# Logits in column quarters behind the turn, 0/1 products in column halves, a reordered start

One NeuronCore of one Trainium2 chip. The metric is device time in microseconds (us), lower is better. The experiments ran on two chips, called 2 and 3 here; which chip the first runs of the kernel before and the changed one used is not on record (it is called the first). On chips 2 and 3 these two kernels took 0.7 to 0.9% longer, so kernels are compared on one chip, or by their ratio to the kernel before on the same chip.

The profiler names the engines: PE is TensorE, which multiplies matrices (PEld its loads of the stationary side), DVE is VectorE, ACT is ScalarE, POOL is GpSimd, SP issues transfers (DMA). "The array" is PE's array. A row "PE sc <- DVE pr: 2.0, 2, 1.7" means that PE products into `sc` waited for DVE's `pr` for 2.0 us in all, 2 times, 1.7 us at the longest; a bracket "[1.71 <-DVE pr]" is the engine's idle time just before a row and what ended it.

## The reference

```python
# attention: B=8, H=8, S=576, head 64; heads 0-3 a window of 32, heads 4-7 every 4th of 128
scores = where(mask, q @ k.T / 8, -1e9);  x = softmax(scores) @ v       # x: (8, 576, 512)
# mixture of experts, 8 experts, hidden size 1024
logits = x @ w_gate;  local = sigmoid(x @ w_local)
for each token in order:
    e = argmax(logits) if first of its row or local < 0.5 else the previous token's e
    out = softmax(logits)[e] * (relu(x @ w1[e]) @ w2[e])
```

All products are f32. A token's expert can depend on its predecessors, so the routing of a group (two batch rows, 1152 tokens) is a chain of small steps. They run beside the attention of later groups: as the program is built, each small step is put into a `gap` between pieces of TensorE work, counted in planned us.

## The kernel before

Parts that the change touches (cuts are marked `# ...`):

```python
def load(n):                                 # keys+queries, the mask once, values of head pair n
    nc.sync.dma_start(out=kq, in_=qk[n])
    if not n: nc.sync.dma_start(out=mk, in_=mask)
    nc.sync.dma_start(out=vt[...], in_=v[n]) # ...
def idle():                                  # products of zeros, ahead of scores 0
    zeros = bank([P, 4, P], "idle")
    for i in range(2): nc.tensor.matmul(zeros, lhsT=blank, rhs=...)   # 128x128 by 128x512
idle(); load(0); load(1)                     # ... and idle() once more behind scores 0
def logits(g):                               # three thirds of 384 tokens in three column groups of 32
    lps = [bank([P, NQ], "lp") for _ in range(2)]        # the middle third's two pieces lie in two banks
    for kk in range(DK):
        for lp, b, c, s, z in sorted(parts, ...):
            nc.tensor.matmul(lp[c*LW:(c+1)*LW, ...], lhsT=wg[:, kk], rhs=..., tile_position=(0, c*LW))
    for lp, b, c, s, z in parts: nc.scalar.copy(le[...], lp[...])     # 4 copies
def put(lv, g):                              # places of tokens: product of two 0/1 matrices
    for j in range(NJ):                      # NJ = 9
        nc.tensor.matmul(tp, lhsT=by_place[:, j], rhs=by_tile[:, j], ...)
def gap(us):                                 # "planned work" passes; at most one small step goes in
    gaps[0] += us
    if soon: soon.pop(0)()
    elif waiting and gaps[0] - last[0] >= waiting[0][0]:
        last[0] = gaps[0]; waiting.pop(0)[1]()
def route(g):
    soon.append(lambda: logits(g))
    steps = [(2.0, fresh), (4.0, carry), (2.0, carry_over), (1.2, choose), (2.7, place), (0.8, gate)]
    waiting.extend(...)                      # then table, seek, and for each group mark and put, then gathers
```

A head pair's `scores` are followed by a DVE clamp (`pr`), an ACT exponential, and `values` (`pv`); two pairs are turned (`tp`) and copied by ACT to `xt`, from which the logits are made. Experts: gather (`xg`), transposes (`tp`), hidden layer (`hp`), output (`yp`).

Of the kernel before, what the change touches and what calls it, by code (L numbers as in the profile page):

```python
# [10 lines left out]
F32 = mybir.dt.float32  # L11
BF16 = mybir.dt.bfloat16
# [10 lines left out]
P = 128  # L23
B, H, S, DH = 8, 8, 576, 64
# [4 lines left out]
WIN, DIL = 32, 4  # L29
# [3 lines left out]
QB = 64  # L33
NB = S // QB
KW = QB + WIN
# [6 lines left out]
CH = 2  # L42
# [3 lines left out]
GB = 2  # L46
NG = B // GB
GS = GB * S
TB = 128
NJ = GS // TB  # L50
NC = 3
NQ = GS // NC
LW = 32
# [9 lines left out]
HALF = P // 2  # L63
# [212 lines left out]
def whole(ctx, tc, exact, qk, v, wgl, w1, w2, con, msk, qmk, out, cst, wg, ones, xd, kept, register):  # L276
    nc = tc.nc
    ctx.enter_context(tc.manual_schedule(engines={ET.PE}))

    def pool(name, bufs, **kw):  # L280
        return ctx.enter_context(tc.tile_pool(name=name, bufs=bufs, **kw))
# [4 lines left out]
    once = pool("once", 1)  # L286
# [4 lines left out]
    ins, work, xp, xtp, marks, mp = (pool(name, bufs) for name, bufs in (  # L291
        ("ins", 4 if exact else 5), ("work", 3), ("xp", 4), ("xtp", 3), ("marks", 2), ("mp", 2)))

    def bank(shape, name):
        return banks.tile(shape, F32, name=name, tag="bank")
# [5 lines left out]
    loaded = {}  # L301

    vts = [once.tile([KW, 2, NB, VW], F32, name=f"vt{i}") for i in range(ahead + 1)]
    for vt in vts:
        nc.vector.memset(vt[:WIN, :, 0], 0.0)

    def load(n):
        kq = ins.tile([P, WIN + 2 * S], F32, name="kq")
        vt = vts[n % len(vts)]
        nc.sync.dma_start(out=kq, in_=qk[n])  # L310
        if not n:
            nc.sync.dma_start(out=mk, in_=mask)
        nc.sync.dma_start(out=vt[WIN:].rearrange("p u i e -> p (u i e)"), in_=v[n])
        loaded[n] = kq[:, :WIN + S], kq[:, WIN + S:], vt

    def nobody():

# [10 lines left out]
        engine = nc.vector if n >= NPB - 7 else nc.gpsimd  # L328
        engine.tensor_copy(vt[:WIN, :, 1:], vt[QB:, :, :NB - 1])  # L329

    def idle():

        zeros = bank([P, 4, P], "idle")
        for i in range(2):
            nc.tensor.matmul(zeros, lhsT=blank, rhs=blank.unsqueeze(1).to_broadcast([P, 4, P]),  # L335
                             start=True, stop=True, skip_group_check=True)

    if not exact:
        blank = once.tile([P, P], F32, name="blank")
        nc.vector.memset(blank, 0.0)  # L340

        idle()
    mk, mask = once.tile([P, QB + 2 * NB * KW] if exact else [KW, 2 * S], BF16, name="mk"), qmk if exact else msk
    load(0)
    load(1)
    if not exact:
        nc.sync.dma_start(out=cst, in_=con)
        nc.sync.dma_start(out=wg.rearrange("p k e -> p (k e)"), in_=wgl)
# [121 lines left out]
    def logits(g):  # L470

        st = routes[g]

        lps = [bank([P, NQ], "lp") for _ in range(2)]
        parts = []
        for c in range(NC):
            at = [(b, c, max(c * NQ, b * S), min((c + 1) * NQ, (b + 1) * S)) for b in range(GB)]
            parts += [(lp, *p) for lp, p in zip(lps, [p for p in at if p[2] < p[3]])]
        for kk in range(DK):
            for lp, b, c, s, z in sorted(parts, key=lambda p: p[0] is lps[1]):  # L480
                nc.tensor.matmul(lp[c * LW:(c + 1) * LW, s - c * NQ:z - c * NQ], lhsT=wg[:, kk],  # L481
                                 rhs=st["xt"][b][:, kk // CH, s - b * S:z - b * S, kk % CH], start=(kk == 0),
                                 stop=(kk == DK - 1), skip_group_check=True, tile_position=(0, c * LW))
        st["le"] = le = sm.tile([NC * LW, NQ], F32, name="le")
        for lp, b, c, s, z in parts:
            w = slice(c * LW, (c + 1) * LW)
            nc.scalar.copy(le[w, s - c * NQ:z - c * NQ], lp[w, s - c * NQ:z - c * NQ])

    def fresh(g):

# [249 lines left out]
    def loads(lv):  # L740

        return 2 if lv == len(GROUPS) - 1 else TW
# [18 lines left out]
    def put(lv, g):  # L761

        by_place, by_tile = tiles.pop("marks")
        nt = COLS[lv]
        tp = bank([P, loads(lv), nt], "put")
        for j in range(NJ):
            nc.tensor.matmul(tp, lhsT=by_place[:, j], rhs=by_tile[:, j], start=(j == 0), stop=(j == NJ - 1))  # L767
        if not g:
            tiles["there", lv] = once.tile([P, loads(lv), nt], F32, name=f"there{lv}")
            nc.vector.tensor_copy(tiles["there", lv], tp)  # L770
        else:
            nc.vector.tensor_tensor(tiles["there", lv], tiles["there", lv], tp, op=Alu.add)
        if g < GROUPS[lv] - 1:
            return
        for w, (what, nobody) in enumerate((("tok", N), ("gate", 0), ("plain", ROWS), ("dilated", ROWS))):
            tiles[what, lv] = to = (kept[what] if loads(lv) == 2
                                    else once.tile([P, nt], I32 if nobody else F32, name=f"{what}{lv}"))
            if w < loads(lv):
                nc.vector.tensor_scalar(to, tiles["there", lv][:, w], float(nobody), None, Alu.add)
        if loads(lv) == 2:  # L780
            rows(lv)
        named[0] = NT if lv else EARLY
# [33 lines left out]
    def pieces(a, z):  # L816
        order = [(t, second) for t in range(a, z) for second in (False, True)]

        for t in (ps[1] + 1 for _, _, ps in TILES if len(ps) > 1):
            if a <= t < z - 1:  # L820
                i = order.index((t, True))
                order[i:i + 2] = order[i + 1], order[i]
        return [(*k, c) for k in order for c in range(PC)]

    needs = pieces(0, TILES[LAST][2][0])
# [3 lines left out]
    def fetch(most):  # L829
        for _ in range(min(most, len(needs))):  # L830
            t, second, _ = needs[0]
            if t >= known[0] or (t >= 2 and t - 2 not in (outs if second else hid)):
                return
            weights(*needs.pop(0))

    def weights(t, second, c):

        if not second and not c:
            at = t - EARLY * (t >= EARLY)
            ev[t] = nc.values_load(tiles["experts", int(t >= EARLY)][0:1, at:at + 1], engines=[ET.SP], min_val=0, max_val=E - 1,  # L840
                                   skip_runtime_bounds_check_because="clamped to the experts")
        w, s, pattern = ((w2, w2s, "p m f -> p (m f)") if second else (w1, w1s, "p m k f -> p (m k f)"))
        cond = {} if t < 2 else dict(cond=ev[t] != ev[t - 2], cond_hint=False)
        m = FK // PC
        nc.sync.dma_start(out=s[t % 2][:, c * m:(c + 1) * m].rearrange(pattern),
                          in_=w[bass.ds(ev[t], 1), c].rearrange("o p x -> (o p) x"), **cond)


    gaps, sent = [0.0], {}
# [98 lines left out]
    waiting, last, soon = [], [0.0], []  # L948

    def gap(us):  # L950
        gaps[0] += us
        if soon:
            soon.pop(0)()
        elif waiting and gaps[0] - last[0] >= waiting[0][0]:
            last[0] = gaps[0]
            waiting.pop(0)[1]()

    def route(g):

        soon.append(lambda: logits(g))  # L960
        steps = [(2.0, fresh), (4.0, carry), (2.0, carry_over), (1.2, choose), (2.7, place), (0.8, gate)]
        lv = GROUPS.index(g + 1) if g + 1 in GROUPS else None
        if lv is not None:
            steps.insert(5, (0.0, lambda g: table(lv)))
            steps.append((1.2, lambda g: seek(lv)))

        waiting.extend((us if g + 1 == GROUPS[0] else 2 * us, lambda f=f: f(g)) for us, f in steps)
        if lv is not None:
            for h in range(g + 1):
                waiting.append((2.5, lambda h=h: mark(lv, h)))  # L970
                waiting.append((6.5 if h else 9.0, lambda h=h: put(lv, h)))
            waiting.extend((1.2, lambda t=t, kk=kk: begin(t, kk))
                           for t in range(EARLY * lv, EARLY * lv + 3) for kk in range(DK))
# [27 lines left out]
    begun = [0]  # L1001
# [14 lines left out]
    for n in range(NPB + 2):  # L1016
        if n < NPB:
            overlap(n)
            (scores_exact if exact else scores)(n)
            if not n and not exact:  # L1020
                idle()
        gap(0.9)
        step()
        if n >= 2 and n % 2 == 1:
            turn((n - 3) // 2)
            if n >= 3 and (n - 3) // 2 % (2 * GB) == 2 * GB - 1:
                route((n - 3) // 2 // (2 * GB))
            gap(0.8)
        if 1 <= n <= NPB:
            values(n - 1)  # L1030
            gap(0.6)
        step()
        if n + ahead < NPB:
            load(n + ahead)
        fetch(1 if not begun[0] else 6)
        if n == NP:
            nobody()
        if n >= 3 and n % 2 == 1:
            store((n - 3) // 2)
        step()  # L1040
# [75 lines left out]
```

## Time and profile before

| kernel before, first chip | |
|---|---|
| median of runs | 726.13 us (724.15 to 727.18, four runs) |
| profiled run | 727.98 us, span 726.2 us |
| TensorE (PE) busy | 709.1 us, 98% |
| attention and start | to 148.6 us; the first expert's hidden layer starts there |
| experts alone | a tile each 14.45 us, to 718 us; then the last write |

In a profile a product's row lasts to the modelled end of its pipeline, so starts of instructions tell more than busy shares (in the profile before, rows of L931 last 593 ns in the mean, and start 429 ns apart in the median): what a piece of work costs the array is the time from its first start to the first start of the next piece. A stop of PE measured by starts is likewise some 0.2 us longer than the idle time in a bracket (1.9 and 1.71 us for the same stop below).

### The profile page before, as it was taken

The page shows a single profiled execution, that of the slowest core. Times are in us where ns is not written, and L with a number is a line of the kernel's source. Part 1 is how long each engine was busy: PE and PEld are TensorE (multiplying, and loading weights), DVE is VectorE, ACT ScalarE, POOL GpSimd, SP SyncE. Part 2 cuts the span into 40 slices and gives each one's busy share as a digit, 9 for nine tenths or more (in the row PEclk, how much of TensorE's full clock was granted, in tenths as well). Part 3 has the DMA queues.
Part 4 walks back from the last instruction along what each step waited for, and adds up shares of the span by engine and source line. Part 5 has one row for each costly group of instructions (what it writes and reads, how often), then busy time and mean ns, then how long its engine had stood idle before and what let it go on. Part 6 is the DMA issues. An engine that isn't in the chain of part 4 may idle for free.

```text
span 726.2 us, 16502 instructions
## 1 busy us (share of the span) xinstructions
PE 709.1 (98%) x6354; PEld 536.4 (74%) x6354; DVE 191.4 (26%) x554; ACT 124.2 (17%) x233; POOL 211.3 (29%) x219
## 2 busy tenths in 40 slices
PE   8999999999999999999999999999999999999995
PEld 6978787967677777667766776677667767776773
DVE  3657597742239212110010101010110101010100
ACT  2646554512000000000100000001000000000000
POOL 2222210342332324313233323332333233323100
PEclk9999999999999999999999999999999999999998
DMA  9969787951683772535594171630169116211780
GB/s 335 338 235 328 230 285 300 402 217 59 185 312 107 229 267 44 162 130 178 176 318 158 53 256 33 203 110 29 33 210 325 38 33 213 100 30 36 216 297 15
DMA packets 37590, 131.22 MB, mean 181 GB/s; under 512 B 6686, under 2 KB 6814, under 8 KB 37504
## 3 DMA queue, kind: packets, MB, share of 16 engines
q1 hardware_dynamic: 29600, 110.68, 43.2%
q0 software_dynamic: 7904, 19.41, 9.6%
q8 instruction: 52, 0.85, 0.5%
q14 instruction: 34, 0.28, 0.1%
HBM read 207.37 MB, written 19.69 MB: 313 GB/s over the span
## 4 chain that ended last, share of the span: by engine, by line
PE 90%; DVE 5%; ACT 1%; issue 1%; DMA 1%; POOL 0%; POOLq 0%; DVEq 0%; ACTq 0%
PE hp L903 34%; PE yp L931 33%; PE sc L373 6%; PE pv L426 4%; PE tp L873 2%; PE hp L897 2%; PE lp L481 2%; PE yp L927 2%; PE put L767 2%; PE tp L452 2%; DVE pr L380 1%; DMA xg<-xd,dilated 1%; PE idle L335 1%; DVE x L432 0%; DVE by_place L749 0%
## 5 line engine op out<-in xcount | busy, mean ns | idle before, releaser
L903 PEld LDWEIGHTS hp<-xe,w1s 128*128 128x128 f32 x2304 | 262.9, 192 | 16.6 <-issue 16.3
L903 PE MATMUL hp<-xe,w1s 128*128 128x128 f32 x2304 | 264.8, 275 | 0.9 <-DVE xe L875 0.9
L931 PE MATMUL yp<-w2s,h 128*128 128x512 f32 x576 | 254.3, 593 | 0.0
L931 PEld LDWEIGHTS yp<-w2s,h 128*128 128x128 f32 x576 | 106.2, 190 | 118.2 <-issue 118.1
L856 POOL DMA_INDIRECT xg<-xd,plain x76 | 73.2, 964 | 296.8 <-PE yp L931 248.3
L907 ACT ACTIVATE h<-hp 128x512 f32<-128x512 f32 x76 | 45.4, 597 | 509.3 <-PE hp L903 481.1
L856 POOL DMA_INDIRECT xg<-xd,dilated x76 | 73.0, 961 | 57.4 <-PE yp L931 51.7
L939 DVE TENSOR_SCALAR y<-yp,gate 128x512 f32<-128x512 f32 x38 | 28.5, 751 | 216.4 <-PE yp L931 102.9
L875 DVE COPY xe<-tp 128x512 f32<-128x512 f32 x38 | 26.2, 690 | 214.6 <-PE tp L873 214.6
L940 POOL DMA_INDIRECT out_dram<-y,tok x38 | 38.7, 1019 | 79.3 <-DVE y L939 75.8
L373 PE MATMUL sc<-kq 64*96 64x64 f32 x1152 | 59.2, 252 | 2.5 <-DVE pr L380 1.8
L373 PEld LDWEIGHTS sc<-kq 64*96 64x96 f32 x1152 | 53.5, 165 | 8.0 <-DVE pr L380 2.7
L380 DVE SCALAR_TENSOR_TENSOR pr<-sc,mk 96x640 f32<-96x640 f32 x64 | 47.8, 747 | 40.7 <-PE pv L426 21.4
L383 ACT ACTIVATE pr<-pr 96x640 f32<-96x640 f32 x64 | 43.8, 685 | 61.3 <-DVE pr L380 56.7
L329 POOL COPY vt<-vt 32x1040 f32<-32x1040 f32 x25 | 26.1, 1045 | 75.1 <-DMA vt<-in_v_dram 62.5
L426 PE MATMUL pv<-vt,pr 96*64 96x65 f32 x1152 | 43.6, 225 | 0.5 <-ACT xt L457 0.2
L426 PEld LDWEIGHTS pv<-vt,pr 96*64 96x64 f32 x1152 | 37.5, 137 | 7.1 <-issue 3.8
L432 DVE TENSOR_TENSOR x<-pv,rec 128x320 f32<-128x320 f32 x64 | 26.9, 453 | 0.2
L873 PE MATMUL tp<-cst,xg 128*128 128x128 f32 x152 | 23.3, 275 | 0.8 <-DMA xg<-xd,dilated 0.8
L452 PE MATMUL tp<-cst,x 128*128 128x128 f32 x144 | 19.2, 278 | 0.0
L873 PEld LDWEIGHTS tp<-cst,xg 128*128 128x128 f32 x152 | 17.6, 141 | 1.9 <-DMA xg<-xd,dilated 1.1
L463 ACT COPY xt<-tp 128x288 f32<-128x288 f32 (+2 forms) x48 | 18.4, 564 | 0.9 <-PE tp L452 0.8
(178 smaller groups left out, 240.5 us busy)
## 6 DMA issues: line engine op xcount, KB each, us to landing
w1s<-in_w_dram SPq DMA_DIRECT2D x160, 512.0 KB
w2s<-in_w_dram SPq DMA_DIRECT2D x160, 512.0 KB
kq<-in_qk_dram SPq DMA_DIRECT2D x32, 592.0 KB
vt<-in_v_dram SPq DMA_DIRECT2D x32, 292.5 KB
xd<-x SPq DMA_DIRECT2D x16, 576.0 KB
xg<-xd,plain POOLq DMA_INDIRECT x76, 2.9
xg<-xd,dilated POOLq DMA_INDIRECT x76, 2.7
out_dram<-y,tok POOLq DMA_INDIRECT x38, 4.2
```

Of the source, the lines that this page charges most:

```text
L373: here[:] = [nc.tensor.matmul(sc[:KW, u, (i - a) * QB:(i - a + 1) * QB], lhsT=kt[h, i * QB:i * QB + KW], rhs=qt[h, i * QB:(i + 1) * QB], s ...
L380: nc.vector.scalar_tensor_tensor(pr[:, :, :w], sc[:KW, :, :w], -CEIL, mk[:, at:at + w].unsqueeze(1).to_broadcast([KW, 2, w]), Alu.max, Alu ...
L383: nc.scalar.activation(pr[:, :, :w], pr[:, :, :w], Act.Exp, scale=SCALE)
L426: here[:] = [nc.tensor.matmul(pv[u * QB:(u + 1) * QB, i - a], lhsT=pr[:, u, (i - a) * QB:(i - a + 1) * QB], rhs=vt[:, u, i], start=True, s ...
L452: nc.tensor.transpose(tp[:, :, i], x[:, c * w + i].rearrange("p g d -> p (g d)"), ident)
L856: i = nc.gpsimd.indirect_dma_start(out=xg[t][:, kk], out_offset=None, in_=xd if full == ROWS else xd[:full], in_offset=bass.IndirectOffset ...
L873: nc.tensor.transpose(tp[:, kk], x[:, kk], ident)
L903: here[:] = [nc.tensor.matmul(hp[:, m], lhsT=w1s[ps[0] % 2][:, at, kk], rhs=x[:, kk], start=(kk == 0), stop=(kk == DK - 1))]
L907: nc.scalar.activation(ht[t][:, half * FK // 2:(half + 1) * FK // 2], hp, Act.Relu)
L931: here[:] = [nc.tensor.matmul(yp, lhsT=h[:, m], rhs=w2s[ps[0] % 2][:, m], start=(m == 0), stop=(m == FK - 1))]
L939: nc.vector.tensor_scalar(y, yp, of_tile("gate", t), None, Alu.mult)
L940: nc.gpsimd.indirect_dma_start(out=out, out_offset=bass.IndirectOffsetOnAxis(ap=of_tile("tok", t), axis=0), in_=y, in_offset=None, bounds_ ...
```

## The change

The intent: make small products shorter (logits in four equal column quarters and one bank; 0/1 products as two column halves), move the logits and all later routing steps behind the ACT copies they wait for, start with a longer run of zeros and with second keys ahead of first values, and hold back weights that no one needs before the first expert. Its core:

```diff
-        idle()                                   # 2 products
+        for i in range(3): nc.tensor.matmul(idle, ...)
-    load(0); load(1)
+    load_keys(0); (mask); load_keys(1); load_values(0); load_values(1)
-            if not n and not exact: idle()       # behind scores 0
 def logits(g):
-        lps = [bank([P, NQ], "lp") for _ in range(2)]   # thirds, 4 pieces
+        m = GS // 4; lp = bank([P, m], "lp")            # quarters of 288
+            for c in range(4): nc.tensor.matmul(lp[c*LW:(c+1)*LW], ..., tile_position=(0, c*LW))
-        4 copies of 384 or 192 columns to le
+        6 copies of 288, 96 or 192 columns to le
 def put(lv, g):
-            nc.tensor.matmul(tp, lhsT=by_place[:, j], rhs=by_tile[:, j], ...)
+            for h in (0, HALF):
+                nc.tensor.matmul(tp[h:h+HALF], lhsT=by_place[:, j, h:h+HALF], rhs=by_tile[:, j], ...,
+                                 tile_position=(0, h))
 def gap(us):
-        if soon:
+        if soon and gaps[0] >= soon[0][0]:
 def route(g):
-        soon.append(lambda: logits(g))
+        logits(g)                                # and route itself is put off:
+        if not waiting: last[0] = gaps[0]        # so fresh comes 2 or 4 us of planned work later
-                route(...)
+                soon.append((gaps[0] + 1.5, lambda g=...: route(g)))
-        fetch(1 if not begun[0] else 6)
+        if begun[0] or needs[0][:2] <= (1, False): fetch(6 if begun[0] else 1)
```

More of the change, by code (lines that the diff above doesn't have):

```diff
@@ L305, in whole, with load_keys, load_values @@
         nc.vector.memset(vt[:WIN, :, 0], 0.0)
-    def load(n):
-        kq = ins.tile([P, WIN + 2 * S], F32, name="kq")
-        vt = vts[n % len(vts)]
-        nc.sync.dma_start(out=kq, in_=qk[n])
-        if not n:
-            nc.sync.dma_start(out=mk, in_=mask)
-        nc.sync.dma_start(out=vt[WIN:].rearrange("p u i e -> p (u i e)"), in_=v[n])
-        loaded[n] = kq[:, :WIN + S], kq[:, WIN + S:], vt
+    def load_keys(n):
+        kq = ins.tile([P, WIN + 2 * S], F32, name="kq")
+        nc.sync.dma_start(out=kq, in_=qk[n])
+        loaded[n] = kq[:, :WIN + S], kq[:, WIN + S:], vts[n % len(vts)]
+    def load_values(n):
+        nc.sync.dma_start(out=loaded[n][2][WIN:].rearrange("p u i e -> p (u i e)"), in_=v[n])
+    def load(n):
+        load_keys(n)
+        load_values(n)
     def nobody():
@@ L329, in overlap @@
         engine.tensor_copy(vt[:WIN, :, 1:], vt[QB:, :, :NB - 1])
-    def idle():
-        zeros = bank([P, 4, P], "idle")
-        for i in range(2):
-            nc.tensor.matmul(zeros, lhsT=blank, rhs=blank.unsqueeze(1).to_broadcast([P, 4, P]),
-                             start=True, stop=True, skip_group_check=True)
     if not exact:
@@ L340, in whole @@
         nc.vector.memset(blank, 0.0)
-        idle()
-    mk, mask = once.tile([P, QB + 2 * NB * KW] if exact else [KW, 2 * S], BF16, name="mk"), qmk if exact else msk
-    load(0)
-    load(1)
+        idle = bank([P, 4, P], "idle")
+        for i in range(3):
+            nc.tensor.matmul(idle, lhsT=blank, rhs=blank.unsqueeze(1).to_broadcast([P, 4, P]),
+                             start=True, stop=True, skip_group_check=True)
+    load_keys(0)
+    mk = once.tile([P, QB + 2 * NB * KW] if exact else [KW, 2 * S], BF16, name="mk")
+    nc.sync.dma_start(out=mk, in_=qmk if exact else msk)
+    load_keys(1)
+    for n in range(2):
+        load_values(n)
     if not exact:
@@ L472, in logits @@
         st = routes[g]
-        lps = [bank([P, NQ], "lp") for _ in range(2)]
-        parts = []
-        for c in range(NC):
-            at = [(b, c, max(c * NQ, b * S), min((c + 1) * NQ, (b + 1) * S)) for b in range(GB)]
-            parts += [(lp, *p) for lp, p in zip(lps, [p for p in at if p[2] < p[3]])]
+        m = GS // 4
+        lp = bank([P, m], "lp")
         for kk in range(DK):
-            for lp, b, c, s, z in sorted(parts, key=lambda p: p[0] is lps[1]):
-                nc.tensor.matmul(lp[c * LW:(c + 1) * LW, s - c * NQ:z - c * NQ], lhsT=wg[:, kk],
-                                 rhs=st["xt"][b][:, kk // CH, s - b * S:z - b * S, kk % CH], start=(kk == 0),
+            for c in range(4):
+                b, s = divmod(c * m, S)
+                nc.tensor.matmul(lp[c * LW:(c + 1) * LW], lhsT=wg[:, kk],
+                                 rhs=st["xt"][b][:, kk // CH, s:s + m, kk % CH], start=(kk == 0),
                                  stop=(kk == DK - 1), skip_group_check=True, tile_position=(0, c * LW))
         st["le"] = le = sm.tile([NC * LW, NQ], F32, name="le")
-        for lp, b, c, s, z in parts:
-            w = slice(c * LW, (c + 1) * LW)
-            nc.scalar.copy(le[w, s - c * NQ:z - c * NQ], lp[w, s - c * NQ:z - c * NQ])
+        edges = sorted({c * m for c in range(5)} | {c * NQ for c in range(NC)})
+        for s, z in zip(edges, edges[1:]):
+            c, d = s // m, s // NQ
+            nc.scalar.copy(le[d * LW:(d + 1) * LW, s - d * NQ:z - d * NQ], lp[c * LW:(c + 1) * LW, s - c * m:z - c * m])
     def fresh(g):
@@ L766, in put @@
         for j in range(NJ):
-            nc.tensor.matmul(tp, lhsT=by_place[:, j], rhs=by_tile[:, j], start=(j == 0), stop=(j == NJ - 1))
+            for h in (0, HALF):
+                nc.tensor.matmul(tp[h:h + HALF], lhsT=by_place[:, j, h:h + HALF], rhs=by_tile[:, j], start=(j == 0),
+                                 stop=(j == NJ - 1), tile_position=(0, h), skip_group_check=True)
         if not g:
@@ L951, in gap @@
         gaps[0] += us
-        if soon:
-            soon.pop(0)()
+        if soon and gaps[0] >= soon[0][0]:
+            soon.pop(0)[1]()
         elif waiting and gaps[0] - last[0] >= waiting[0][0]:
@@ L958, in route @@
     def route(g):
-        soon.append(lambda: logits(g))
+        logits(g)
+        if not waiting:
+            last[0] = gaps[0]
         steps = [(2.0, fresh), (4.0, carry), (2.0, carry_over), (1.2, choose), (2.7, place), (0.8, gate)]
@@ L1019, in whole @@
             (scores_exact if exact else scores)(n)
-            if not n and not exact:
-                idle()
         gap(0.9)
@@ L1026, in whole @@
             if n >= 3 and (n - 3) // 2 % (2 * GB) == 2 * GB - 1:
-                route((n - 3) // 2 // (2 * GB))
+                soon.append((gaps[0] + 1.5, lambda g=(n - 3) // 2 // (2 * GB): route(g)))
             gap(0.8)
@@ L1034, in whole @@
             load(n + ahead)
-        fetch(1 if not begun[0] else 6)
+        if begun[0] or needs[0][:2] <= (1, False):
+            fetch(6 if begun[0] else 1)
         if n == NP:
```

## The prediction

> **What bounds the kernel now.** I read the page first: busy time by engine, the slices, and the chain of work that ended last.
>
> ```profile
> PE 709.1 (98%) x6354; PEld 536.4 (74%) x6354; DVE 191.4 (26%) x554; ACT 124.2 (17%) x233; POOL 211.3 (29%) x219
> PE   8999999999999999999999999999999999999995
> PE hp L903 34%; PE yp L931 33%; PE sc L373 6%; PE pv L426 4%; PE tp L873 2%; PE hp L897 2%; PE lp L481 2%; PE yp L927 2%; PE put L767 2%; PE tp L452 2%; DVE pr L380 1%; DMA xg<-xd,dilated 1%; PE idle L335 1%; DVE x L432 0%; DVE by_place L749 0%
> ```
>
> PE, the TensorE matmuls, is busy from end to end, and 67% of the span is the experts' products (L903, L931), which the change leaves alone. So time can only come from products that get shorter, or from stretches in which PE stands still. The view of waits, for PE and then for its weight loads, says how little of the second kind is on record:
>
> ```profile
> PE sc L373 <- DVE pr L380: 1.8, 4, 0.8
> PE lt L496 <- ACT le L487: 1.7, 2, 0.8
> PE hp L903 <- DVE xe L875: 0.9, 1, 0.9
> PE tp L873 <- DMA xg<-xd,dilated: 0.8, 1, 0.8
> ...
> PEld lp L481 <- ACT xt L463: 3.3, 8, 0.7
> ```
>
> The last line is worth more than it looks. A matmul row's duration runs to the modelled end of the product, so a busy PE can hide a wait. I therefore read the places of the change in the timeline, by the starts of instructions. First the start of the kernel:
>
> ```profile
> 1.91 3.78 PE L335 MATMUL idle<-blank 128*128 128x512 f32 x4 [1.91 <-DVE blank L340]
> 5.62 3.15 PE L373 MATMUL sc<-kq 64*96 64x64 f32 x36
> 8.70 3.22 PE L335 MATMUL idle<-blank 128*128 128x512 f32 x4
> 11.85 1.75 PE L373 MATMUL sc<-kq 64*96 64x64 f32 x36
> 13.52 1.27 PE L426 MATMUL pv<-vt,pr 96*64 96x65 f32 x36
> ```
>
> Each f32 product is two instructions. The same 36 score instructions take 3.15 us at 5.62 and 1.75 us at 11.85; a zero product of 512 columns starts 0.85 us after the last at 1.91, and later 128x512 products (L931) 0.43 us apart. The array runs at half rate until about 11.2 us, and the first values start at 13.52. Then the first logits, with the instructions after them:
>
> ```profile
> 42.50 2.33 ACT L463 COPY xt<-tp 128x288 f32<-128x288 f32 x6
> 42.54 3.88 PE L481 MATMUL lp<-xt,wg 128*32 128x384 f32 x32
> 43.42 1.16 PEld L481 LDWEIGHTS lp<-xt,wg 128*32 128x32 f32 x14 [0.73 <-ACT xt L463]
> 44.88 0.82 PEld L481 LDWEIGHTS lp<-xt,wg 128*32 128x32 f32 x12 [0.31 <-ACT xt L463]
> 46.35 0.80 PE L426 MATMUL pv<-vt,pr 96*64 96x65 f32 x20
> ```
>
> The weight loads stop twice for ACT's copies of the turned features, which last until 44.83. Lastly the chain in order of time, for the 0/1 products (put, whole columns) and a hidden layer that is in column halves already (L897):
>
> ```profile
> 119.88 2.14 PE put L767 x18
> 131.43 2.13 PE put L767 x18
> 232.70 2.19 PE put L767 x18
> 245.90 1.95 PE put L767 x18
> 258.92 1.95 PE put L767 x18
> 271.44 1.95 PE put L767 x18
> 325.89 7.62 PE hp L897 x256
> ```
>
> [...] in the first logits three instructions of 384, 192 and 384 columns in three column groups start within 14 ns of each other; and L897 starts an instruction each 7.62/256 = 30 ns, while put needs 1.95/18 = 108 ns or more. [...] from the last half-column product to the first whole one at 341 us there is about 0.1 us beyond the product's own time, and the first pair starts late by some 0.05 us more. [...]
>
> **The change part by part.**
>
> *Start.* Before: four instructions of zeros, scores 0, four more of zeros, scores 1, values 0 at 13.52. After: six instructions of zeros, 6 x 0.854 = 5.12 us, from 1.91 to 7.04. [...] Scores 0 then run from 7.04 to about 8.95 (some ten instructions at half rate, the rest 42 ns apart). Scores 1 need the two buffers of scores 0, each given back by a DVE row of 0.82 and 0.69 us: 9.4 to 11.0. The keys of pair 1 landed at 7.9 us and now pass 293 KB of values at 400 KB/us, so about 7.2: not in the way. Values 0 start at 11.0 in place of 13.52: **-2.5 us**. The keys of pairs 2 and 3 land at about 11.0 and 13.2 us, wanted at about 12.2 and 15: just in time.
>
> *0/1 products.* In halves, 36 instructions start as 18 pairs, 58 ns apart as in L897: 1.05 us in place of 2.0. In the four products amid the experts a change of mode each way costs about 0.3 us together: 2.0 - 1.35 = 0.66 each, 2.6 in all. The two amid the attention follow or precede work in column halves (pv), so changes of mode fall away: from the last instruction before to the first after they take 2.28 and 2.31 us, after the change about 1.1 and 1.3: 2.2. Sum **-4.8 us**.
>
> *Logits.* Now 3.81, 3.80, 3.34 and 3.47 us from the first to the next instruction (14.4). Alone, four quarters of 288 columns in four column groups need 8 instructions of each group, 8 x 0.255 = 2.04 us (0.24 us of streaming, plus what three groups lost today: 338 ns for 320), plus 0.1. But the first three come one half of the values (0.75 us) after the turn, at 43.3 us in the example, and the second half of the features is copied only at 44.83: two passes, a wait of some 0.4, two passes, about 2.7 us. So I take 1.1 us each for three, 1.3 for the fourth: -4.6; a further change of mode, as they now stand inside the values, costs back 0.4. **-4.2 us.**
>
> *Delay of the routing behind the logits.* Its first transposes (L496) twice ran into the ACT copies; from the streaming end of the work before, PE stood 1.0 us both times. They now come 2 to 4 us of planned work later: **-2.0 us**. Six copies instead of four on ACT (0.14 us fixed cost each by the rows of 468 and 309 ns) add 0.3 us four times, mostly beside other work: +0.3.
>
> *Fetches held back.* The second weights of tile 1 (2 MB, 5 us at 400 GB/s) no longer go before the first expert, when the DMA engines are full (share 1.02 from 130 to 150 us). The first gather can land sooner. PE lost about 2.0 us there (0.98 for the gather, 1.04 for DVE's copy right behind it), but where the pieces fall is new: **-0.7 us**.
>
> Sum: -2.5 - 4.8 - 4.2 - 2.0 + 0.3 - 0.7 = -13.9. I give back 0.4 us for waits on DVE where PE now arrives sooner (its share is 90% from 90 to 110 us): 726.5 - 13.5 = **713.0 us**.
>
> **Rivals.** (a) *DVE becomes the bound of the attention.* Against: 16.5 of 20 us at 50 to 70, so there is room outside 90 to 113 us. For: PE already stands some 3 us for L380 between 103 and 114. Then savings before about 115 us (start, logits, some 8 us) are partly eaten: 716 to 719. (b) *Column groups do not run fully at once*[...]. For: three lose 5%. Against: L897 and L927 keep two at full rate. If four groups do no better than two, the logits gain 1 us instead of 4: 716. (c) *The clock stays low longer*, as scores 0 and 1 no longer have zeros between them: then scores 1 and values 0 run at half rate and the start gains nothing: 715.5. (d) *All waits vanish*: logits at 2.1 us each, no gap at the first expert, as the intent has it: 709.
>
> **Range and chances.** The parts are independent and each is bounded by rows in the trace; most of the sum is shorter PE time in a kernel bound by PE. Adding rivals gives 709 to 717.5. The line of 2% is at 712.0, one microsecond under my number, so it is nearly even; I lean to within 2%, as sums of small gains tend to be collected short: 0.41 faster, 0.58 within, 0.01 slower.
>
> **What would show it.** In the changed profile: values 0 (L426) starting near 11.0 us; put's 36 instructions in 1.1 to 1.4 us; lp's 32 instructions in 2.1 to 2.8 us with weight loads waiting less for ACT; no wait of lt for le; the experts' tile period unchanged (14.45 us). Wrong would be: lp still over 3.3 us, put near 2 us, half-rate scores after 8 us, or new waits on L380 that add up to over 3 us.

## The result

Median 715.5 us (713.95 to 716.1, four runs). The ratio to the kernel before is 0.9853, 95% interval 0.9826 to 0.9881. Ratios here are the mean time of one kernel's fast runs over that of the other's of the same rounds, so not quite the ratio of the medians. By this ratio the gain is 10.7 us, inside the range, in the class "within 2%". The two profiles are 14.0 us apart (726.2 and 712.2), which is more: the profile before was of the slowest run of its kernel (727.98 us), the one after of the fastest (713.95 us). All runs are marked as fast in the record. Much of what follows is about why single runs differ.

The page after, busy time by engine:

```profile
PE 695.4 (98%) x6460; PEld 527.5 (74%) x6460; DVE 194.8 (27%) x554; ACT 125.1 (18%) x241; POOL 211.2 (30%) x219
```

PE is still the bound and lost 13.7 us of busy time. The timeline of the start (start, duration, engine, instruction):

```profile
1.91 4.24 PE L341 MATMUL idle<-blank 128*128 128x512 f32 x6 [1.91 <-DVE blank L336]
6.08 1.75 PE L376 MATMUL sc<-kq 64*96 64x64 f32 x36
9.74 1.27 PE L429 MATMUL pv<-vt,pr 96*64 96x65 f32 x36
11.61 1.75 PE L376 MATMUL sc<-kq 64*96 64x64 f32 x36 [0.60 <-DVE rec L434]
```

The first scores run at full rate already; the record of the array's clock has the rise from half to full rate at 4.8 us, against 11.2 before. Values 0 start at 9.74 (13.52 before), scores 2 at 11.61 (14.72 before). Now the first logits, in the timeline, and three of the 0/1 products, in the chain of work that ended last, in order of time:

```profile
39.94 1.16 PEld L481 LDWEIGHTS lp<-xt,wg 128*32 128x32 f32 x20 [0.19 <-ACT xt L466]
39.94 2.69 PE L481 MATMUL lp<-xt,wg 128*32 128x288 f32 x32
41.42 0.65 PEld L481 LDWEIGHTS lp<-xt,wg 128*32 128x32 f32 x12 [0.32 <-ACT xt L466]
```

```profile
113.39 1.03 PE put L770 x36
123.22 1.18 PE put L770 x36
225.19 1.20 PE put L770 x36
```

From the first start of a piece to the next piece, the four logits took 14.4 us before and 2.61 + 2.24 + 2.18 + 2.17 = 9.2 after; the six 0/1 products 12.15 before and 1.13 + 1.07 + 4 x 1.19 = 6.96 after. The longest waits of PE:

```profile
PE sc L376 <- DVE pr L383: 2.0, 2, 1.7
PE tp L455 <- DVE x L435: 1.4, 1, 1.4
PE hp L907 <- DVE xe L879: 1.3, 1, 1.3
```

The wait of the routing's first transposes for ACT (`lt`, the transposed logits, for `le`, their copy: 1.7 us before) is gone. In its place DVE stops the array: all PE waits for DVE in this view, without the first zeros', were 3.0 us before and are 5.3 now. The scores' part hardly grew (1.8 to 2.0 us), but it came in 4 stops of 0.8 us at most and comes in 2, one of 1.7. All listed waits together are 6.6 us before and 6.7 after: the gain is shorter work on PE, and waiting has only moved. One is worth a look, on DVE and PE near 103 us:

```profile
101.73 1.35 DVE L750 TENSOR_TENSOR by_place<-cst,at 128x1152 f32<-128x1152 f32 x1
103.58 0.77 DVE L758 TENSOR_TENSOR by_tile<-there,cst 128x99 f32<-128x99 f32 x4
104.60 1.40 DVE L383 SCALAR_TENSOR_TENSOR pr<-sc,mk 96x640 f32<-96x640 f32 x2
105.45 1.75 PE L376 MATMUL sc<-kq 64*96 64x64 f32 x36 [1.71 <-DVE pr L383]
```

The 0/1 matrices are built ahead of the clamp `pr` that frees the score buffers, and PE stands 1.9 us by starts. What comes next shows in a table by stretches (stretch, length, busy us of PE, PEld, DVE, ACT and POOL with counts, granted clock, DMA share, GB/s):

```profile
103.50:107.10 3.60, 1.89 (x46) 1.71 (x40) 3.60 (x13) 1.26 (x2) 0.00 (x0) 1.00 1.02 414
107.20:110.50 3.30, 3.30 (x29) 2.87 (x29) 2.53 (x3) 2.79 (x7) 0.00 (x0) 0.50 1.02 346
110.60:114.00 3.40, 3.40 (x76) 2.12 (x78) 1.85 (x6) 1.77 (x6) 0.00 (x0) 1.00 1.03 418
```

For 3.4 us behind the idle stretch the array is granted half its clock: nine transposes that take 1.13 us elsewhere take 2.11 there, and 1.7 us are lost. The profile before has no such stretch.

The other new wait, at 80.6 us, has a different origin, on POOL and DVE:

```profile
79.64 1.04 POOL L332 COPY vt<-vt 32x1040 f32<-32x1040 f32 x1 [4.79 <-DMA vt<-in_v_dram]
79.67 1.10 DVE L509 TENSOR_TENSOR eq<-eq,cst 128x72 f32<-128x72 f32 x1
```

L509 takes 0.23 us elsewhere, and here ends 0.09 us after POOL's copy. In the three profiles of this kernel the row took 1.10, 1.03 and 0.91 us beside such a copy and ended within 0.1 us of the copy's end, while L435 (`x` from `pv` and `rec`) takes 0.41 us (rows of 256 elements) with such a copy and without. Why the copy draws out the one row and not the other is not shown. The routing steps, moved, now meet that copy, and the turn behind them waits 1.4 us (1.6 by starts).

### The profile page after: what moved, and what is told of

It reads as the page before. It is cut to its first block, busy times and chain, and to the rows that moved or that the text cites. A ratio compares the mean times of both kernels' runs of the same rounds, so it can differ in the third digit from the quotient of the medians.

```text
span 712.2 us, 16720 instructions
## 1 busy us (share of the span) xinstructions
PE 695.4 (98%) x6460; PEld 527.5 (74%) x6460; DVE 194.8 (27%) x554; ACT 125.1 (18%) x241; POOL 211.2 (30%) x219
## 4 chain that ended last, share of the span: by engine, by line
PE 94%; DVE 4%; ACT 1%; issue 0%; POOL 0%; POOLq 0%; DVEq 0%
PE hp L907 36%; PE yp L935 35%; PE sc L376 6%; PE pv L429 4%; PE tp L877 2%; PE tp L455 2%; PE hp L901 2%; PE yp L931 2%; DVE pr L383 1%; PE lp L481 1%; PE put L770 1%; PE idle L341 1%; DVE x L435 1%; ACT pr L386 0%; ACT xt L466 0%
## 5 line engine op out<-in xcount | busy, mean ns | idle before, releaser
L376 PE MATMUL sc<-kq 64*96 64x64 f32 x1152 | 57.2, 248 | 3.2 <-DVE pr L383 2.0
L435 DVE TENSOR_TENSOR x<-pv,rec 128x320 f32<-128x320 f32 x64 | 27.0, 454 | 0.2
L455 PEld LDWEIGHTS tp<-cst,x 128*128 128x128 f32 x144 | 16.3, 146 | 2.7 <-DVE x L435 1.8
```

What stands on the lines that cost most here:

```text
L376: here[:] = [nc.tensor.matmul(sc[:KW, u, (i - a) * QB:(i - a + 1) * QB], lhsT=kt[h, i * QB:i * QB + KW], rhs=qt[h, i * QB:(i + 1) * QB], s ...
L435: nc.vector.tensor_tensor(x[:, a:z, n % 2], pv[:, :, :DH], r.unsqueeze(2).to_broadcast([P, z - a, DH]), op=Alu.mult)
L455: nc.tensor.transpose(tp[:, :, i], x[:, c * w + i].rearrange("p g d -> p (g d)"), ident)
```

## The experiments

Each kernel was timed in five rounds against the kernel before, plus its profiled run; all gave correct results. Means are of these six runs. "Mean clock" is the granted share of the array's clock that each run reports. It counts the time before the first rise as full (the view gives 1.00 for the first 10 us of the kernel before), so it shows later stretches at half rate only, and those after the last product.

| kernel | chip | mean us | of before | mean clock |
|---|---|---|---|---|
| changed (a_control) | 2 | 720.8 | 0.9851 | 0.9937 |
| 0/1 products whole (a_whole_put) | 2 | 725.9 | 0.9929 | 0.9915 |
| old start (a_old_start) | 2 | 720.9 | 0.9864 | 0.9938 |
| logits in thirds (a_thirds) | 2 | 722.4 | 0.9884 | 0.9927 |
| changed (a_again) | 3 | 720.8 | 0.9848 | 0.9918 |
| idle places filled (a_fill) | 3 | 719.7 | 0.9821 | 0.9972 |
| logits at the turn (a_at_turn) | 3 | 721.8 | 0.9854 | 0.9958 |
| fetches not held (a_no_hold) | 3 | 720.7 | 0.9836 | 0.9937 |
| first routing step at once (a_fresh_now) | 3 | 729.9 | 0.9980 | 0.9860 |
| idle time taken away (p_all) | 3 | 717.2 | 0.9789 | 0.9945 |
| the same, later second step (p_late) | 3 | 718.8 | 0.9811 | 0.9942 |
| p_late with the old start (p_old_start) | 3 | 720.5 | 0.9845 | 0.9925 |

The intervals of the ratios are some 0.003 to each side, 2 us; by the spread of the runs, the difference of two kernels here is uncertain by 1 to 3.5 us, and one under 1 us says nothing. On chip 3 the kernels from a_fill to a_no_hold and p_all were of one call and the others of another; the kernel before had 732.6 and 732.0 us there.

**The changed kernel again.** No edit.

> The changed kernel itself, once more. Theory: the two profiles (726.2 and 712.2 us of span, 14.0 apart) differ by more than the medians (10.6 apart) because the moment at which the array's clock rises is not fixed: the profile before had it at 11.2 us, the one after at 4.8 us and a half-rate stretch from 107 to 111 us. So this run should again be 10 to 11 us under the kernel before in its mean, with single runs spread over 2 to 3 us, and its profile should show another moment of the rise. Rival: the profile after is typical and the first runs were not; then the mean difference is near 14 us.

The ratio is the same, 0.985, so the 14.0 us between the two first profiles is not typical. Single runs lie between 717.4 us (mean clock 0.998) and 725.1 us (0.988). Its profile, of 724.07 us, shows a half-rate stretch in another place, again in the table by stretches:

```profile
66.40:69.80 3.40, 2.21 (x54) 2.08 (x54) 1.95 (x6) 0.83 (x2) 1.05 (x1) 1.00 0.89 314
69.90:79.90 10.00, 10.00 (x103) 8.41 (x103) 4.02 (x11) 4.38 (x10) 2.10 (x2) 0.50 0.50 178
80.10:84.00 3.90, 3.90 (x79) 2.87 (x71) 1.42 (x4) 1.98 (x7) 0.00 (x0) 1.00 0.17 22
```

PE stood 1.36 us by starts at 66.4 us (a wait for nothing that the profile shows), and 10.2 us at half rate followed, worth 5 us. Half of the expectation fell: the rise at the start was at 5.0 us, as in the first profile; it is the later stretch that made this run slow. The kernel's other repeat (a_again) gave 0.9848, as expected.

**0/1 products whole.** The products of `put` as before.

> The changed kernel with the 0/1 products in whole columns again. Theory (the array is the bound, every product made shorter counts in full): 5 us slower than the changed kernel (12.15 us of the six products in the trace before against 6.96 after). Rival: the two products amid the attention stand next to waits on DVE, which take their part; then only the four amid the experts count, 3 us.

5.1 us slower, as the theory had it. In its profile the six products take 12.06 us by starts, the two amid the attention 2.13 each against 1.13 and 1.07. The times alone do not exclude the rival's 3 us, though: the mean clock of these runs was lower too (0.9915 and 0.9937, some 1.6 us by an estimate from these shares), and the difference is uncertain by 3 us.

**Old start.**

```diff
-    load_keys(1); load_values(0); load_values(1)
+    load_values(0); load(1)
-        for i in range(3):          # zeros
+        for i in range(2):          # and two more behind scores 0
```

> The changed kernel with the old start: two products of zeros, scores 0, two products of zeros, and first values ahead of second keys. Theory: 3 us slower in the mean (the profiles have scores 2 at 14.72 and 11.61 us), with a spread of its own, since a rise of the clock in the first zeros shortens the old start too. Rival: the profile before caught an unusually late rise, and the old start costs 1.5 us or less in the mean.

0.1 us slower. In its profile the clock rose at 4.7 us and scores 2 came at 12.66 us, 0.9 behind the changed kernel's 11.78. The profile before, with its rise at 11.2 us, was not typical: the rival holds here. The new start's lead is partly lost again: ahead of scores 2 PE waits 0.7 us for the keys' transfer in a_control and 1.0 us for DVE in a_again. (More in the last experiment.)

**Logits in thirds.** The products and copies of before, in the new place.

> The changed kernel with the logits in thirds and two banks again, at the new place behind the turn. Theory: the place already takes most waits away and thirds need 16 instructions of 192 columns one after another in the middle column group, 16 x 0.168 = 2.7 us, so each logits takes about 2.9 us against 2.3: 2 to 2.5 us slower than the changed kernel in all. Rival: it is the four column groups that bring the whole gain, and thirds cost 5 us.

1.6 us slower, near the theory, though uncertain by 3 us; the rival's 5 us falls. The four logits take 3.24 + 2.88 + 3.15 + 2.85 = 12.1 us in its profile against 10.2 in a_control's. By these rows the place took 14.4 to 12.1, the four column groups the rest.

**Idle places filled.**

```diff
+        if n == 25: filler(2)       # products of zeros ahead of scores 25
         scores(n)
+        if n == 19: filler(1)
...
             features(0)
+            filler(1)
```

> The changed kernel with products of zeros put where every profile of it has the array idle in the attention: two ahead of scores 25 (1.9 us of waiting for DVE), one after scores 19 (1.4 to 1.6 us), one behind the first expert's transposes (1.4 to 2.0 us). Nothing else is taken away. Theory: [...] with the idle time filled the half-rate stretches at 105 to 112 and 143 to 150 us are gone from the profile, the mean clock of the runs is up by 0.002 to 0.004, and the mean time is 1 to 3 us under the changed kernel's (ratio to the kernel before 0.982 to 0.984 in place of 0.985). Rival: the stretches have nothing to do with idle time; then they stay, and the time is the same or longer by the 1 to 2 us that zeros add.

No half-rate stretch is left in its profile, all six runs have a mean clock of 0.996 to 0.998, and their spread is 1.5 us. Two stretches of a_again and the same two of a_fill, in the table by stretches:

```profile
100.00:125.00 25.00, 23.29 (x500) 20.57 (x500) 20.74 (x58) 13.27 (x28) 0.00 (x0) 0.93 1.01 389
125.00:150.00 25.00, 22.17 (x326) 20.42 (x321) 12.23 (x31) 8.59 (x17) 10.66 (x11) 0.93 0.88 333
```

```profile
100.00:125.00 25.00, 24.00 (x465) 19.60 (x461) 21.14 (x61) 13.24 (x28) 0.00 (x0) 1.00 0.97 364
125.00:150.00 25.00, 23.28 (x380) 20.97 (x376) 13.57 (x34) 9.31 (x18) 10.71 (x12) 1.00 0.95 365
```

Work that is of no use was added and nothing was taken away, and the time fell by 1.1 us (0.9848 to 0.9821, another call); this gain is within the noise. The clock is clearer: all 6 runs are at 0.996 or more, against 3 of the 12 of the changed kernel (a_control and a_again). So in these runs filling the places kept the clock up; the rival would have had the stretches stay. One profile without them would not show it: a_old_start and a_no_hold have none either.

A stop alone does not decide it, though. In all 14 profiles, half-rate stretches between the start and the last product begin and end a whole number of steps of 3.41 us after the first rise. There are 14 of them, and each follows a step with PE idle for 1.1 us or more; but 15 other steps with 1.1 to 1.9 us idle were not followed by one.

**Logits at the turn.**

```diff
-                soon.append((gaps[0] + 1.5, lambda ...: route(g)))
+                soon.append((gaps[0], lambda ...: route(g)))
```

> The changed kernel with the quartered logits right behind the turn (at the next point between pieces of work) in place of 1.5 us of planned work later. Theory: their bank and the second half of the features come from ACT's copies, so each of the first three waits 0.5 to 1 us more: 1.5 to 2.5 us slower. Rival: one bank in place of two was enough, and the place does nothing: within 0.7 us.

The logits do take longer, 3.47 + 3.38 + 3.03 + 3.14 = 13.0 us with waits for ACT, as the theory had it. But the kernel is only 1.0 us slower. The waits of scores and turns for DVE are 0.6 and 1.1 us in its profile, against 2.0 and 1.4 in the changed kernel's: all routing came earlier and met other scores. So by single profiles the 1.5 us of delay won some 3 us at the logits and gave about 2 of them to DVE later. The runs can't confirm this split: their mean clock was higher too (0.9958 and 0.9918).

**Fetches not held.** The condition on `fetch` removed.

> The changed kernel with the second weights of tile 1 fetched ahead of the first expert again. Theory: the gathers of tile 0 land later behind 2 MB, and the first expert's transposes wait up to 1 us: 0 to 1 us slower. Rival: the gathers have slack, no difference beyond 0.7 us.

No difference (720.7 and 720.8) beyond the noise. This part of the change does nothing for the time that these runs can show.

This profile also shows why runs of one kernel differ. Its scores 25 wait 1.72 us for DVE, as the changed kernel's do (1.71), but the stop lies across the border of two steps of 3.41 us, and no half rate follows:

```profile
103.47:106.88 3.41, 2.79 (x72) 2.58 (x71) 3.41 (x14) 0.63 (x1) 0.00 (x0) 1.00 1.02 417
106.89:110.29 3.40, 2.32 (x42) 2.25 (x43) 3.37 (x9) 1.31 (x3) 0.00 (x0) 1.00 1.02 416
```

In the first profile of the changed kernel it lay within one step (103.74 to 107.15, 1.7 us idle), and half rate followed. Of the seven profiles of a_ kernels and the changed one with this stop, four have 1.4 to 1.7 us of it in one step and half rate behind it; three have at most 1.1 us in any step and none. At the first expert idle time does not separate the cases (1.5 to 2.1 us in a step followed four times, 1.6 to 1.9 us not followed four times), and near 80 us none of seven steps with 1.2 to 1.4 us was followed. What decides there is not tested here.

**First routing step at once.**

```diff
-        if not waiting: last[0] = gaps[0]
-        steps = [(2.0, fresh), ...
+        steps = [(0.0, fresh), ...
```

> The changed kernel with the first routing step at the next point behind the logits, in place of 2 to 4 us of planned work later. Theory of the prediction: its transposes run into ACT's six copies again, about 1 us twice or more, so 2 to 3 us slower than the changed kernel. Rival, after the run with the logits at the turn (which took 3 us more for logits and no more time in all): the earlier place moves the DVE bursts away from where they stop the array, and that pays the wait back; within 1 us of the changed kernel.

9.1 us slower: both expectations missed. The waits of its profile, then the table by stretches:

```profile
PE lt L497 <- ACT le L488: 2.8, 2, 1.4
```

```profile
43.60:47.40 3.80, 2.40 (x51) 2.08 (x48) 2.17 (x12) 1.75 (x7) 0.47 (x1) 1.00 0.60 183
47.60:54.20 6.60, 6.60 (x79) 6.27 (x75) 3.84 (x12) 2.90 (x5) 1.99 (x2) 0.50 0.76 245
```

The transposes now wait for six copies, not four: by starts, PE stands 1.6 us twice (1.0 before the change). Behind the first wait come 6.8 us at half rate, 3.4 us lost. The runs' mean clock is 0.986 against 0.992, some 4 us of 715. Waits and clock make about 7 of the 9 us (an estimate from these rows and shares); what the rest is stays open. Within this kernel, the run with the lowest clock (0.978) took 736.7 us and the one with the highest (0.990) 726.6.

**Idle time taken away.**

```diff
-    waiting: mark (2.5), put (6.5 or 9.0)
+    waiting: by_place (2.5), by_tile (3.0), put (3.5 or 6.0)
-    steps = [(2.0, fresh), (4.0, carry), ...
+    steps = [(2.0, fresh), (1.0, fresh_rest), (3.0, carry), ...
+    if not begun[0] and 0 in xe and gaps[0] - turned_at[0] < 1.0: return False   # first expert not yet
```

> The changed kernel with the idle time itself taken away: the building of the 0/1 matrices in two steps 3 us of planned work apart in place of one burst on DVE, the first routing step in two as well, and the first expert not begun until some attention work has gone in between its transposes and its first products. Theory: of the 1.9, 1.5 and 1.4 us of idle PE time most is won, and half-rate stretches behind them too: 3 to 6 us under the changed kernel, 0.977 to 0.981 of the kernel before. Rival: the DVE work only moves and meets other score products; then it is within 1 us of the changed kernel.

717.2 us, 0.9789 (0.9754 to 0.9823): 3.6 us under the changed kernel on the same chip (in another call; by the ratios 4.3), and the lowest mean of this study. It is 15.5 us under the kernel before. The three edits were not tried one by one, and the profiles of the p_ kernels also lack a stop of about 1 us near 279 us that all profiles of the a_ kernels have, so what part of the gain each brings is open. The first expert's wait is gone, filled with values (timeline, PE):

```profile
140.73 0.66 PE L892 MATMUL tp<-cst,xg 128*128 128x128 f32 x4
141.32 0.80 PE L429 MATMUL pv<-vt,pr 96*64 96x65 f32 x20
...
143.27 0.94 PE L922 MATMUL hp<-xe,w1s 128*128 128x128 f32 x6
```

In a_again the hidden layer started 1.7 us after the transposes had ended, with nothing between. The wait for DVE at 80 us fell from 1.6 to 0.6 us by starts. The one of scores 25 stayed at 1.9 us: both DVE steps still fell in one head pair.

**The same, later second step.** 4.5 us of planned work between the two DVE steps.

> The version with the idle time taken away, with the second step of the 0/1 matrices 4.5 us of planned work behind the first in place of 3. In the last version the two DVE steps still fell in one pair, and scores 25 waited 1.9 us. Theory: the wait is gone or under 0.8 us, and with it the half-rate stretch behind it: 1 to 3 us under the last version, so 0.975 to 0.978 of the kernel before, and 5 to 8 us under the changed kernel on the same chip. Rival: the wait moves to another pair; then 0.979 as the last version.

718.8 us, 0.9811, and 2.0 us under the changed kernel in place of 5 to 8. The wait of scores 25 fell to 0.75 us, but 1.5 us came up in the middle of the next scores and 1.0 us at a turn; half-rate stretches are still in the profile (112.8 to 119.7). The rival holds: the DVE work moved and met other scores.

**The same with the old start.**

> The same version with the old start (two products of zeros, scores 0, two more, first values ahead of second keys). With less idle time later on, less noise from the clock. Theory: the new start is worth 1 to 2 us in the mean (0.9 us of scores 2 where both starts had an early rise of the clock, 3.1 us where the old one had a late rise). Rival: nothing, as in the run of the changed kernel with the old start (0.1 us).

1.7 us slower than p_late, as the theory had it, though the intervals (0.978 to 0.984 and 0.981 to 0.988) overlap. With the 0.1 us of the first such pair, the new start is worth about 1 us, uncertain by 2; neither pair shows the 2.5 us of the prediction.

## Why the prediction was right, and where its steps were off

| step | predicted | rows of the two traces | undone on the chip |
|---|---|---|---|
| start | -2.5 | -3.1 (scores 2), with a late rise before | +0.1, +1.7 |
| 0/1 products | -4.8 | -5.2 | +5.1 (some 1.6 of it clock) |
| logits: quarters and place | -4.2 | -5.2 | +1.6 (thirds), +1.0 (at the turn) |
| routing behind the logits | -2.0 | two waits of 1.0 us gone | +9.1 |
| fetches held back | -0.7 | idle behind the first gather 2.0 to 1.5 us | -0.1 |
| given back | +0.4 for DVE waits, +0.3 for ACT's two more copies | +2.3 for DVE waits (3.0 to 5.3), 1.7 for 3.4 us at half rate | -3.6 when partly taken away |

**Right**: the whole lies in the range, and the mechanism of the main terms was right: PE is the bound, shorter products shorten the kernel, and column groups run at once (the four instructions of a pass of the logits start within 20 ns of each other in the median of the profile after). The 0/1 products are the cleanest: 4.8 us was read off a hidden layer in column halves, the rows have 5.2, and undoing them cost 5.1 with the reserve made above. That 13.5 us came out as 10.7 and no worse is partly luck: the start and the DVE term were both sized in the gain's favour, and the routing's delay, worth more than its 2.0, made part of it good. Rival (b) falls: four column groups need 2.17 us where nothing is waited for, by the row's starts, close to the 2.14 of the text. For two groups the profile before has the numbers: at L927 a pair of 128x512 products starts every 0.43 us, as one whole-column product does at L931, and at L897 a pair of 128x64 ones every 0.06 us, against 0.11 us for one of 128x128 at L903.

**The start was too large**: 2.5 us predicted, about 1 us on the chip. The step that failed took the rise at 11.2 us, read off one profile, for the start of every run of the kernel before. With the old start the rise came at 4.7 and 6.8 us in two other profiles. The ten instructions of scores 0 at half rate behind the six zero instructions were the author's estimate; no trace before the change shows when the rise comes there, and in the profile after all 36 run at full rate (1.75 us). Rival (c) fell too: the clock never stayed low longer, with rises from 4.8 to 7.9 us in all profiles with the new start.

**The term for DVE was too small**: +0.4 us. The argument "16.5 of 20 us at 50 to 70, so there is room" is an average. What stops the array is a burst of 1 to 3 us of routing steps ahead of one clamp or turn, and the new order put two such bursts where PE waits for them: 1.6 us near 80 us and 1.9 us at 103.5 (by starts). The second is rival (a) in the place that it named (103 to 114), the first in another. The text had PE stand some 3 us there for L380 in the old kernel; the view has 1.8 us in the whole kernel. (Its range, too, ends at 717.5 us where its own rival (a) goes to 719.) And it is paid twice, which no rival had: such a stop can be followed by 3.41 us or more at half rate, 1.7 us lost each time. Filling the stops kept the clock up (mean 0.9972, against 0.9918); that the same stop is followed by half rate in one run and not in another (mean clock 0.988 to 0.998 within one kernel) is part of why runs differ. It is not why the two first profiles are 14.0 us apart and the kernels 10.7: the profile before has no such stretch and the one after has one. Of these 3.3 us the late rise before makes some 2.1 (scores 2 at 14.72 us, against 12.6 and 12.7 in two profiles of the old start with an early rise); the rest is open.

**The routing's delay was too small as a single term**: it was sized with the four copies of before. With the six that the quarters need, leaving it out costs 9.1 us. Terms of a change that lean on one another can't be summed from the side of the old kernel alone: the undone parts add to some 17 us, and the change gives 10.7.

The fetches' term is nothing, within the noise. What stays open: some 2 us of the 9.1; and on chips 2 and 3 PE also stands up to 1.6 us near 279 us, in the experts, for nothing the profile shows, which the first two profiles and those of the p_ kernels do not have.

## What to carry to other kernels

Here the array was the bound (98% busy), and splitting small products into column groups paid: the six 0/1 products went from 12.15 to 6.96 us, and the four logits, moved as well, from 14.4 to 9.2. The first of these gains could be read beforehand from the spacing of a similar product in the same trace (L897, 30 ns an instruction). When work is moved to avoid one wait, look at which queue it joins: here the 1.7 us of waiting for ACT went, and 2.3 us more of waiting for DVE came, in bursts ahead of the instruction that the array needs; and a stop of 1.2 to 1.7 us was followed by 1.7 us or more lost in clock in some runs. Before trusting one profile of such a kernel, compare its clock record with another run's, and break up bursts rather than only moving them.

## What the profiles show of the clock and of four column groups

- PE idle for 1.2 to 1.7 us of a stretch of 3.4 to 3.8 us (busy 1.89 of 3.60, 2.21 of 3.40, 2.40 of 3.80 us) was followed by half rate for 3.4, 10.2 and 6.8 us, and products of zeros in such places kept the clock up (mean 0.9972, against 0.9918).
- Idle time alone does not decide here (14 steps with 1.1 us or more followed by half rate, 15 not). An estimate from the same 14 profiles does better: count each product of a 3.41 us step by its streamed columns, times the share of the array's rows and columns that it uses. All 11 steps under 1300 of these were followed by half rate, none of those over 1540, and 3 of the 18 between. No run tests this.
- With score products between two pairs of zero products the rise came 9.3 us after the first product once (first product at 1.9, rise at 11.2) and 2.8 and 4.9 us in two other profiles, and 2.8 to 6.0 us with six zero instructions in a row. What made the one rise late is open.
- The quarter of the logits in columns 96 to 127 gave correct results in every experiment that has it, and the four instructions of a pass start within 20 ns of each other in the median of the profile after (up to 0.27 us where one waits).
